# Attention, routed experts and a two-layer network on one core: the product of the last 64 keys with V in two column halves

## The chip, the cores and the metric

The kernel runs on one core of a Trainium2 chip. The metric is the device time of one execution in microseconds; the time before is the median of three runs, 412.99 us (412.54 to 413.68). A profile of one further execution was taken by the hardware profiler, and all rows below come from it. The engines are named as the profile names them: PE is TensorE's matmul, PEld its weight load, DVE is VectorE, ACT is ScalarE, POOL is GpSimd, SP is SyncE, which issues most of the DMAs.

## The reference

Three stages follow each other. The change lies in the first.

```python
# attention, B = 2, H = 8 heads, S = 576 positions, D = 64
scores = scale * np.matmul(q, k.transpose(0, 1, 3, 2)) + bias   # bias: a small network of the relative position
attn = np.exp(scores - np.max(scores, axis=-1, keepdims=True))
attn = attn / (np.sum(attn, axis=-1, keepdims=True) + 1e-09)
x = np.matmul(attn, v)            # 576 keys: 4 blocks of 128 and a tail of 64
# a top-1 mixture of 8 experts with a capacity, then x -> leaky relu(x @ w_in) @ w_out
```

## The kernel before

**Units.** The attention is cut into 40 units: batch b, block c of 128 queries (c = 0 to 3, and c = 4 for the last 64 queries) and pair p of heads 2p and 2p+1. Four units, p = 0 to 3, make one block. The order of the blocks is written out by hand, as is the order of everything else: each engine runs its instructions in the order in which the code issues them.

**The loop.** Step n of the loop (line 1270) issues on PE: `s0(n+1)`, the scores of the next unit (`qk`, L333, into St); `tr(n)`, the transposes of the exponentials A of unit n (L366 for the four full key blocks, L370 for the 64 tail keys of both heads together); one bias matmul group (L182, four column groups of 32 into pb) as long as there are any; the pieces that finish a block (`fin_b`, L441 and L449 behind the fourth unit, `fin_c`, L458 one step later); then `pv(n-1)`, the product with V of the unit before; then, in the earlier steps, another bias group. DVE adds bias and scores and takes the extreme (`ttr`, L345, into sv), ACT takes the exponential (`expo`, L356), and DVE and ACT copy the transposes out of PSUM (`tr_evac`, AT and AX_). AT and AX_ of a unit are made one whole step before its `pv`.

**The bias.** The bias matmuls end in bs, which SP stores to memory (L222, scr) and loads back skewed as bt (L314), which `ttr` reads. The bias groups run out on the way: PE starts the last one at 114.1 us.

**The product with V.** For c < 4 the result xp of a unit is 128 x 128: head 2p in PSUM partitions 0 to 63, head 2p+1 in 64 to 127. The four full key blocks are eight matmuls of 64 columns, one for each head and block (L403), whose weights are a head's 64 columns of V. The tail is one matmul over all 128 columns (L399): AX_ holds the 64 tail keys of both heads interleaved in its 128 partitions, and vd holds V's tail rows spread the same way, with zeros where the other head's keys are. Each matmul in fp32 is two passes on PE, so the profile shows L399 as x2 and L403 as x16 in each unit. There are 32 units with c < 4. The other 8 (c = 4, L407 and L409) are not touched.

Of the kernel before, what the change touches and what calls it, by code (L numbers as in the profile page):

```python
# [26 lines left out]
NFULL = S // 128  # L27
# [47 lines left out]
def tile_attention_moe_mlp(ctx, tc, qc, kc, vc, wpk, cst, ctok, cap, wm, wo, out):  # L75
    nc = tc.nc
# [318 lines left out]
    def pv(c, p, ATs, Vs, xp):  # L395
        V, vt, vd = Vs
        AT, AX_ = ATs
        if c < NFULL:
            nc.tensor.matmul(xp[:, p, :], vd[:, p], AX_, start=True, stop=False)  # L399
            for t in range(NFULL):  # L400
                for j in range(2):
                    h = 2 * p + j
                    nc.tensor.matmul(xp[64 * j : 64 * j + 64, p, :], V[:, t, 64 * h : 64 * h + 64],  # L403
                                     AT[:, j, 128 * t : 128 * t + 128], start=False, stop=t == NFULL - 1)
        else:
            for t in range(NFULL):
                nc.tensor.matmul(xp[:, p, :], V[:, t, 128 * p : 128 * p + 128], AT[:, 0, 128 * t : 128 * t + 128],  # L407
                                 start=t == 0, stop=False)
            nc.tensor.matmul(xp[:, p, :], vt[:, 128 * p : 128 * p + 128], AX_[0:64], start=False, stop=True)  # L409
# [860 lines left out]
    for n in range(N + 1):  # L1270
# [9 lines left out]
        if n + 1 < N:  # L1280
            b, c, p = units[n + 1]
# [12 lines left out]
        if n >= 1:  # L1294
            b, c, p = units[n - 1]
            pv(c, p, ATt.pop(n - 1), Vt[b], xpt[b, c])
            if p == NP - 1:
                fa = (b, c) + fin_a(c, rst[b, c], xpt[b, c], n == N)
# [71 lines left out]
```

## Time and profile before

| | |
|---|---|
| median of three runs | 412.99 us (412.54 to 413.68) |
| the profiled execution, its own time | 412.21 us |
| its span, first to last instruction | 410.3 us |
| TensorE busy | 381.2 us, 93% |
| VectorE busy | 309.2 us, 75% |
| ScalarE busy | 241.3 us, 59% |
| L399 / L403 | 32 x 2 and 32 x 16 passes, between 42.8 and 205 us |

A busy PE in this profile is not a PE at its peak: rows overlap, and the time that a group takes is best read as the distance from its first start to the start of what follows it. A row of the timeline merges instructions of one line that stand in a row; its first two columns are the start and how long it lasts, xN is how many passes it holds, and a bracket is the idle time before it and what ended that.

### The profile page before, as it was taken

To read this page: it belongs to the slowest core of one execution; us is meant where nothing else is said; L and a number is where in the kernel's file an instruction comes from. 1 tells how busy PE (TensorE), PEld (TensorE's weight loads), DVE (VectorE), ACT (ScalarE), POOL (GpSimd) and SP (SyncE) were. 2 spreads that over 40 slices of the span, in tenths; PEclk is the share of its full clock that TensorE was granted. 3 is DMA by queue.
4 is the path that set the end of the run, shared out by engine and by line. 5 is a ranking of instruction groups with operands and counts; after the bars stand their busy time and mean duration, and the time that the engine had idled before them with its cause. 6 is when DMAs were issued, how large, how long until landed. Compare 5 with 4: busy or idle time off the path is not lost. (4 is left out here: it accounts for less than half of the span.)

```text
span 410.3 us, 8306 instructions
## 1 busy us (share of the span) xinstructions
PE 381.2 (93%) x2926; PEld 316.8 (77%) x2926; DVE 309.2 (75%) x736; ACT 241.3 (59%) x519; POOL 139.4 (34%) x110
## 2 busy tenths in 40 slices
PE   4886999998899999999999999998999999899993
PEld 2244566666588988998988999998998778789872
DVE  5998988799855689799548883128989999999310
ACT  2756897697865777767565785546554222455200
POOL 1444857374300011031241304850233255222311
PEclk9999899999999999999998999999899999999998
DMA  8989599698779847788285189692344366630011
GB/s 194 332 254 334 173 322 326 203 316 270 199 218 320 297 150 224 224 269 196 95 235 208 41 306 366 218 316 81 140 137 172 103 201 206 208 106 1 12 66 51
DMA packets 34370, 82.97 MB, mean 202 GB/s; under 512 B 8491, under 2 KB 8875, under 8 KB 32272
## 3 DMA queue, kind: packets, MB, share of 16 engines
q1 hardware_dynamic: 33200, 79.88, 61.1%
q0 software_dynamic: 1120, 2.48, 1.7%
q8 instruction: 25, 0.41, 0.4%
q14 instruction: 25, 0.20, 0.1%
HBM read 60.29 MB, written 23.20 MB: 203 GB/s over the span
## 5 line engine op out<-in xcount | busy, mean ns | idle before, releaser
L345 DVE CUSTOM_DVE_ANT_0 sv<-St,bt 128x576 f32<-128x576 f32 x72 | 52.9, 750 | 32.9 <-PE St L333 21.9
L677 POOL TENSOR_TENSOR P<-raw,P 128x1024 fp32r<-128x1024 f32 x18 | 45.4, 2523 | 77.4 <-ACT P L676 70.2
L356 ACT ACTIVATE A<-sv,mx 128x576 f32<-128x576 f32 x72 | 59.2, 837 | 3.2 <-DVE mx L345 3.1
L333 PE MATMUL St<-K,Q 128*128 128x320 f32 (+1 forms) x320 | 53.5, 309 | 2.5 <-DVE mx L345 2.4
L182 PE MATMUL pb<-Gt,WP 128*32 128x272 f32 (+17 forms) x352 | 43.1, 509 | 13.2 <-DVE Gt L165 8.4
L333 PEld LDWEIGHTS St<-K,Q 128*128 128x128 f32 x320 | 43.9, 189 | 14.5 <-issue 9.8
L273 POOL TENSOR_TENSOR Q<-qr,Q 128x256 fp32r<-128x256 f32 x22 | 17.0, 772 | 103.0 <-ACT Q L265 63.2
L165 DVE TENSOR_SCALAR Gt<-WL,bp 128x432 f32<-128x432 f32 (+17 forms) x101 | 49.4, 549 | 0.1
L676 ACT CAST P<-raw 128x1024 fp32r<-128x1024 f32 x27 | 28.3, 1048 | 27.8 <-DVE raw L694 22.2
L366 PE MATMUL pt<-CS,A 128*128 128x128 f32 x288 | 41.6, 284 | 1.5 <-ACT A L356 0.8
L376 ACT COPY AT<-pt 128x512 f32<-128x512 f32 x40 | 23.4, 584 | 30.9 <-PE pt L366 30.8
L366 PEld LDWEIGHTS pt<-CS,A 128*128 128x128 f32 x288 | 38.0, 206 | 2.4 <-ACT A L356 1.3
L169 POOL TENSOR_SCALAR Gt<-WL,bp 128x528 f32<-128x528 f32 (+12 forms) x17 | 34.3, 2023 | 9.3 <-PE pb L182 9.2
L182 PEld LDWEIGHTS pb<-Gt,WP 128*32 128x32 f32 x352 | 13.2, 112 | 30.5 <-DVE Gt L165 14.3
L403 PE MATMUL xp<-AT,V 128*64 128x128 f32 x512 | 35.9, 284 | 0.0
L193 ACT ACTIVATE bs<-pb,CS 128x288 f32<-128x288 f32 (+53 forms) x60 | 27.3, 501 | 12.4 <-PE pb L182 7.9
L861 PE MATMUL g<-yhl,P 128*128 128x304 f32 x96 | 30.3, 316 | 2.8 <-DVE gfa L886 2.8
L1198 PE MATMUL ac<-P,hq 128*128 128x512 f32 (+1 forms) x80 | 31.5, 394 | 0.0
L1196 PE MATMUL ac<-P,hq 128*128 128x512 f32 (+1 forms) x80 | 31.5, 394 | 0.0
L1197 PE MATMUL ac<-P,hq 128*128 128x512 f32 (+1 forms) x80 | 31.5, 393 | 0.0
L403 PEld LDWEIGHTS xp<-AT,V 128*64 128x64 f32 x512 | 28.0, 139 | 4.0 <-issue 0.2
L894 DVE TENSOR_TENSOR hq<-gfa,hq 128x304 fp32r<-128x304 f32 x32 | 28.8, 901 | 1.4 <-ACT hq L893 1.4
(322 smaller groups left out, 913.9 us busy)
## 6 DMA issues: line engine op xcount, KB each, us to landing
bt<-scr SPq DMA_DIRECT2D x24, 576.0 KB, 5.7
w<-wo SPq DMA_DIRECT2D x13, 1024.0 KB, 5.1
scr<-bs SPq DMA_DIRECT2D x36, 295.5 KB, 5.0
raw<-wm SPq DMA_DIRECT2D x14, 512.0 KB, 6.5
w<-wm SPq DMA_DIRECT2D x10, 512.0 KB, 5.2
srt<-pre SPq DMA_DIRECT2D x6, 771.0 KB, 9.7
qr<-qc SPq DMA_DIRECT2D x16, 256.0 KB, 5.9
kr<-kc SPq DMA_DIRECT2D x12, 288.0 KB, 7.0
```

Of the source, the lines that this page charges most:

```text
L165: nc.vector.tensor_scalar(G, src, bp[:, g : g + 1], 0.0, op0=ALU.add, op1=ALU.max)
L169: nc.gpsimd.tensor_scalar(G, src, bp[:, g : g + 1], 0.0, op0=ALU.add, op1=ALU.max)
L182: nc.tensor.matmul(pb[32 * q : 32 * q + 32, 0 : hi - lo], W2, gs[:, q, lo:hi], start=True, stop=True)
L333: nc.tensor.matmul(St[:, o + lo : o + hi], Q[:, h - 2 * p, w, :], K[:, h - 2 * p, lo:hi], start=n == 0, stop=n == len(seq) - 1)
L345: nc.vector.tensor_tensor_reduce(out=sv, in0=St, in1=bt[:, jb], scale=-0.125, scalar=3.0e38, op0=ALU.add, op1=ALU.min, accum_out=mx)
L356: nc.scalar.activation(A[:, :, j], sv, AF.Exp, bias=mx, scale=-1.0, accum_out=rs[:, col : col + 1])
L366: nc.tensor.transpose(pt[:, 128 * t : 128 * t + 128], A[:, 128 * t : 128 * t + 128, j], ident)
L403: nc.tensor.matmul(xp[64 * j : 64 * j + 64, p, :], V[:, t, 64 * h : 64 * h + 64], AT[:, j, 128 * t : 128 * t + 128], start=False, stop=t = ...
L677: eng.tensor_tensor(out=P_[:, 1], in0=raw, in1=P_[:, 0].bitcast(F32), op=ALU.subtract)
L1196: nc.tensor.matmul(ps, hh, wh, start=k == 0, stop=False)
L1197: nc.tensor.matmul(ps, hh, wl, start=False, stop=False)
L1198: nc.tensor.matmul(ps, hl, wh, start=False, stop=k == F2 // 128 - 1)
```

## The change

`pv` no longer issues the 128-column tail matmul ahead of the eight others. Behind them it issues two of 64 columns, one for each head: the weights are that head's half of vd's columns, the moving operand is the same AX_ for both, and the result is added to that head's half of xp. The first matmul of each head (key block 0) now starts the sum, and the tail ends it. Nothing else differs on any engine.

```diff
         if c < NFULL:
-            nc.tensor.matmul(xp[:, p, :], vd[:, p], AX_, start=True, stop=False)
-            for t in range(NFULL):
+            for t in range(NFULL + 1):
                 for j in range(2):
                     h = 2 * p + j
-                    nc.tensor.matmul(xp[64 * j : 64 * j + 64, p, :], V[:, t, 64 * h : 64 * h + 64],
-                                     AT[:, j, 128 * t : 128 * t + 128], start=False, stop=t == NFULL - 1)
+                    w, a = (V[:, t, 64 * h : 64 * h + 64], AT[:, j, 128 * t : 128 * t + 128]) if t < NFULL else (vd[:, p, 64 * j : 64 * j + 64], AX_)
+                    nc.tensor.matmul(xp[64 * j : 64 * j + 64, p, :], w, a, start=t == 0, stop=t == NFULL)
```

On PE, in a unit with bias matmuls (the first of the places, at 49 us in the trace), the columns are the line, the operation, out<-in by name, and the shape of the result:

```order
 L182 MATMUL pb<-Gt,WP 32x400 x4
-L399 MATMUL xp<-AX__500,vd_95 128x128
-L403 MATMUL xp<-AT,V 64x128 x8
+L403 MATMUL xp<-AT,V 64x128 x8
+L403 MATMUL xp<-AX__500,vd_95 64x128 x2
 L182 MATMUL pb<-Gt,WP 32x416 x4
 L333 MATMUL St<-K,Q 128x320
```

The 128-column matmul stood between matmuls of 32 and of 64 columns; now the ones of 32 and of 64 columns follow each other directly.

On PE, in a unit without bias matmuls (at 119 us in the trace), before:

```order
L366 MATMUL pt<-CS,A 128x128 x8
L370 MATMUL pt_1606<-CS,A 128x128
L458 MATMUL pl_1625<-CS,lt 128x128
L399 MATMUL xp<-AX__1531,vd_96 128x128
L403 MATMUL xp<-AT,V 64x128 x8
L333 MATMUL St<-K,Q 128x320
```

and the same place in the changed kernel, whose lines behind L399 are one lower (L457 is L458 of before):

```order
L366 MATMUL pt<-CS,A 128x128 x8
L370 MATMUL pt_1619<-CS,A 128x128
L457 MATMUL pl_1638<-CS,lt 128x128
L403 MATMUL xp<-AT,V 64x128 x8
L403 MATMUL xp<-AX__1543,vd_96 64x128 x2
L333 MATMUL St<-K,Q 128x320
```

Here the 128-column matmul followed others of 128 columns; the step from 128 to 64 columns, which came behind it, now comes ahead of the V products.

## Rows read from the trace of the kernel before

**Rows 1.** The page: busy us, share of the span, number of instructions.

```profile
PE 381.2 (93%) x2926; PEld 316.8 (77%) x2926; DVE 309.2 (75%) x736; ACT 241.3 (59%) x519; POOL 139.4 (34%) x110
```

**Rows 2.** Stretches: length, busy us of each engine, granted clock, DMA share, GB/s.

```profile
core 0: us, PE busy (x) PEld busy (x) DVE busy (x) ACT busy (x) POOL busy (x), PEclk, DMA share, GB/s
...
54.00:71.00 17.00, 17.00 (x160) 10.67 (x159) 15.94 (x38) 15.07 (x35) 10.88 (x8) 1.00 0.99 325
...
79.40:111.00 31.60, 27.35 (x265) 19.19 (x266) 31.01 (x86) 26.50 (x60) 16.42 (x14) 1.00 0.87 266
111.00:206.00 95.00, 94.83 (x908) 84.19 (x905) 69.47 (x240) 66.86 (x174) 14.03 (x21) 1.00 0.73 224
```

**Rows 3.** PE timeline of a unit with bias matmuls: start, us, line, operation, count.

```profile
48.51 0.27 PE L370 MATMUL pt<-CS,A 128*128 128x128 f32 x1
48.71 0.88 PE L182 MATMUL pb<-Gt,WP 128*32 128x400 f32 x8
49.52 0.49 PE L399 MATMUL xp<-AX__500,vd 128*128 128x128 f32 x2
49.94 1.09 PE L403 MATMUL xp<-AT,V 128*64 128x128 f32 x16
50.96 0.91 PE L182 MATMUL pb<-Gt,WP 128*32 128x416 f32 x8
```

**Rows 4.** PE timeline of a unit without bias matmuls.

```profile
119.39 0.27 PE L370 MATMUL pt<-CS,A 128*128 128x128 f32 x1
119.49 0.27 PE L458 MATMUL pl<-CS,lt 128*128 128x128 f32 x1
119.60 0.39 PE L399 MATMUL xp<-AX__1531,vd 128*128 128x128 f32 x2
119.92 1.09 PE L403 MATMUL xp<-AT,V 128*64 128x128 f32 x16
```

**Rows 5.** PE by line, 109 to 206 us: busy us, mean ns | idle.

```profile
L403 PE MATMUL xp<-AT,V 128*64 128x128 f32 x336 | 23.0, 279 | 0.0
...
L399 PE MATMUL xp<-AX__1395,vd 128*128 128x128 f32 x2 | 0.5, 326 | 0.0
...
L399 PE MATMUL xp<-AX__1531,vd 128*128 128x128 f32 x2 | 0.4, 275 | 0.0
```

**Rows 6.** PE timeline of the first unit, then the clock granted in stretches.

```profile
42.80 0.80 PE L399 MATMUL xp<-AX__431,vd 128*128 128x128 f32 x2
43.52 1.98 PE L403 MATMUL xp<-AT,V 128*64 128x128 f32 x16
45.43 1.02 PE L182 MATMUL pb<-Gt,WP 128*32 128x464 f32 x8
...
42.20:45.50 3.30, 3.30 (x26) 2.15 (x26) 3.27 (x10) 2.83 (x7) 3.20 (x3) 0.50 0.69 196
219.60:223.00 3.40, 3.40 (x17) 3.33 (x16) 3.21 (x14) 1.26 (x2) 1.02 (x1) 0.51 0.97 379
```

**Rows 7.** Timeline of PE, ACT, SP and DVE: the chain from 68 to 79 us.

```profile
68.62 1.07 PE L182 MATMUL pb<-Gt,WP 128*32 128x512 f32 x8
69.76 0.91 ACT L193 ACTIVATE bs<-pb,CS 128x80 f32<-128x80 f32 x2 [1.51 <-PE pb L182]
70.69 0.32 SPq L222 DMA_DIRECT2D scr<-bs  x1
75.39 1.40 SPq L314 DMA_DIRECT2D bt<-scr  x3
79.43 0.76 DVE L345 CUSTOM_DVE_ANT_0 sv<-St,bt 128x576 f32<-128x576 f32 x1 [2.06 <-DMA bt<-scr]
```

**Rows 8.** Stretches around the store of that chain; then all stores of scr (page, issues).

```profile
57.00:70.00 13.00, 13.00 (x123) 8.21 (x118) 12.94 (x31) 11.15 (x27) 8.86 (x7) 1.00 1.04 347
70.00:72.00 2.00, 2.00 (x21) 1.83 (x23) 0.96 (x4) 1.78 (x4) 2.00 (x1) 1.00 0.62 227
...
scr<-bs SPq DMA_DIRECT2D x36, 295.5 KB, 5.0
```

**Rows 9.** Waits behind 111 us: PE to 206 us, DVE at 164 us, PE behind 205 us.

```profile
PE pt L366 <- ACT A L356: 0.2, 1, 0.2
...
164.34 0.76 DVE L345 CUSTOM_DVE_ANT_0 sv<-St,bt 128x576 f32<-128x576 f32 x1 [0.28 <-PE St L333]
...
PE g L861 <- DVE gfa L886: 2.8, 4, 0.9
```

## Prediction, made before the changed kernel ran

> **What bounds the kernel now.** I read the page first, for the busiest engine. It is PE [rows 1], but a share over the whole span says nothing of one stage, so I next read the stretches of the attention, where the changed matmuls lie. There the reader should see three regimes [rows 2]. From 54 to 71 us PE is never idle, and DVE nearly never. From 79.4 to 111 us DVE is busy 31.01 of 31.60 us and PE only 27.35: PE waits for DVE and ACT there. From 111 to 206 us PE is busy 94.83 of 95 us and DVE 69.47, and the one wait of PE is 0.2 us [rows 9]. So a shorter product with V is worth its full length behind 111 us, nothing between 79.4 and 111, and ahead of that only what reaches the DMA on which the middle stretch hangs. Third I read PE's timeline for what one unit pays [rows 3, 4], and last the chain of that DMA [rows 7].
>
> **What a tail matmul costs now.** I measure from start to start. Neighbouring passes of 128 columns stand (119.60 - 119.39) / 2 = 0.105 us apart [rows 4], but the last one ahead of matmuls of 32 columns takes 0.20 us [rows 3]: a change of width costs 0.095 us. Behind the bias matmuls the tail takes 49.94 - 49.52 = 0.42 us [rows 3]: two passes (0.21), the change of width (0.095) and about 0.11 for a weight load of 128 columns that nothing covers. Behind matmuls of 128 columns it takes 119.92 - 119.60 = 0.32 us [rows 4], which is the same without that load.
>
> **What the two halves cost.** The sixteen passes of 64 columns take 50.96 - 49.94 = 1.02 us. Taking off the change of width behind them (0.095) and half a weight load ahead (0.055, an estimate from the 0.11 for twice the columns) leaves 0.87 us for eight pairs, 0.109 us each: the two heads' passes run side by side. The halves add two pairs, 0.22 us. Upper bound: the halves read the same AX_ columns, which no pair of before does, and should that keep them apart they are four passes, 4 x 0.109 = 0.44 us. Lower bound: below 0.22 there is nothing, since a pair already runs at one 128-column pass. I take 0.22, because everything but the shared operand is as in the sixteen.
>
> Here a rule speaks against the change. The row says that eight pairs with their loads fit in 1.02 us [rows 3]. The Trainium skill, in "TensorE: Matmul & The Clock Gate", Part 3, section The mechanism, says that a weight load overlaps running matmuls only if it goes to other rows of the array. All these loads fill the same rows. By that rule each pair would show its load, 0.109 + 0.055 = 0.164 us, and eight would need 1.31 us; the trace has 1.02 and does not bear it out. I keep it as the fourth rival below.
>
> **The balance of one unit.** Behind matmuls of 32 columns (L182 or L449): minus 0.42, plus 0.22, a gain of 0.20 us. The step from 32 to 64 columns, which takes the place of the step from 32 to 128, has no row; I take the same 0.095 for it, as the steps from 64 to 32 and from 128 to 32 both show, and without it the gain would be 0.295. Behind matmuls of 128 columns the change of width is not saved but moved ahead: minus 0.32, plus 0.095, plus 0.22, which is a gain of 0.005 us, in effect nothing.
>
> **How many of each.** The mean length of L399 tells them apart: 326 ns behind narrow matmuls, 275 ns behind wide ones. Between 109 and 206 us there are 6 of the first kind (the first at 110.34 us, AX__1395) and 15 of the second, 21 units for the 336 passes of L403 [rows 5]. Gain: 6 x 0.20 + 15 x 0.005 = 1.3 us. The cover that could be lost is DVE's slack: in its tightest wait on a gaining unit, at 164.34 us, DVE still idles 0.28 us for PE [rows 9], more than the 0.20. Behind 205 us PE waits only where it and DVE chase each other (2.8 us in four places) [rows 9], and both start from work that PE released, so I let the shift run through to the end.
>
> **Ahead of 79 us.** The first unit runs at half the clock [rows 6]: L399 takes 0.72 us, and two more pairs at twice 0.109 cost 0.44; of the 0.28 I take 0.2, since bias matmuls slide into the slow stretch. Four more units ahead of 68.62 us (the first at 49.52 us [rows 3]) gain 0.20 each, one with wide neighbours nothing. PE is thus 1.0 us early at 68.62 us. From there: bias matmuls, ACT's copy, the store, the load, and DVE's wait of 2.06 us that ends at 79.43 [rows 7]. ACT had waited 1.51 us for PE, so the store is issued 1.0 us earlier. Between the store's issue and the load's lie 4.7 us. The DMA engines were full from 57 to 70 us, at a share of 1.04, and are at 0.62 in the next two [rows 8]. If the store waits behind that backlog, nothing is gained; if not, 1.0 us is. All stores have a median of 5.0 us [rows 8], so 4.7 is no sign of either. I take half, 0.5 us, with 0 and 1.0 as ends.
>
> **From 79.4 to 111 us** four more narrow units gain 0.8 us on PE. I count it at nothing: DVE's 31.01 us of work hide it. If that cover were gone it would be 0.8 us more.
>
> **Waits that move.** L399 was where PE first needed AX_; now the last pair needs it. AX_ was copied one whole step before, so neither waits, and no other queue is touched: no DMA is issued, moved or dropped, and the orders on DVE, ACT, POOL and SP stay as they are. ACT's copy of xp behind the fourth unit waits for the end of `pv`, which comes earlier.
>
> **Sum.** 1.3 + 0.5 = 1.8 us. The profiled execution took 412.21 us, which gives 410.4; the median of the runs is 0.8 us higher, 412.99, and 1.8 us off that is **411.2 us**.
>
> **Rivals.** (1) DVE takes the bound. The early 1.0 us is lost in the DMA backlog, and behind 111 us DVE, at 69.47 of 95 us, fills up around the ends of blocks where it has the most to do; the slack of 0.28 us at 164.34 [rows 9] is not far from 0.20, and a later one may be eaten by what came before. With half of the 1.3 lost as well, 412.4 us. For it: DVE's slack is thin. Against it: PE's single wait of 0.2 us in 95.
>
> (2) The halves do not run side by side, because both draw the same AX_ columns. Then each unit pays 0.44 us for its tail: narrow units lose 0.02, wide ones 0.44 + 0.095 - 0.32 = 0.215, so behind 109 us 15 x 0.215 + 6 x 0.02 = 3.3 us slower, **416.3 us**. It decides from 0.28 us for the two halves up: 6 x (0.42 - x) + 15 x (0.225 - x) is zero there. For it: no pair of before shares its operand. Against it: all other pairs do run together.
>
> (3) The change does not do what it says, the narrow step costing what the wide one did with its load: 413.0 us. Against it: the load of 64 columns takes less in the row of sixteen.
>
> (4) Each added pair shows its load: 0.33 us for the halves, so narrow units gain 0.09 and wide ones lose 0.105, 15 x 0.105 - 6 x 0.09 = 1.0 us slower, 414.0 us. The rule of the skill above would give this; the 1.02 us speak against it.
>
> **How the numbers follow.** My forecast, 1.3 us with an early part between 0 and 1.0 us, has a chance of 0.62, and its own range is 410.6 to 411.8. Rival 1 has 0.26, rival 2 has 0.06, rival 3 has 0.03 and rival 4 has 0.03. The range of 8 in 10 takes in rival 1 and at its lower end a narrow step that costs less than 0.095: 410.3 to 412.6. Where PE falls to half the clock is not mine to place: 219.6 to 223 us ran at 0.51 [rows 6], and a shift of 1.8 us may move such a stretch onto other work; it stays within that range. A difference of over 0.3%, 1.24 us, is about what a measurement of this kernel can tell from no change. Faster by more: 0.60, nearly all of the forecast. Within: 0.33, rival 1, rival 3, rival 4's lower part and the forecast's upper edge. Slower by more: 0.07.
>
> **What would show it.** Right: in units with bias matmuls the distance from the first V pass to the next group grows from 1.02 to 1.24 us, with L182 directly ahead of it; at 119 us PE's distance from L458's successor (L457) to the scores is unchanged within 0.02 us; DVE stays full from 79 to 111 us; and PE's lead at 206 us exceeds its lead at 111 us by 1.3 us. The early part is read at the wait that ended at 79.43: earlier by 0 to 1.0 us. Wrong: twenty passes that take 1.45 us (rival 2), new idle time of PE behind 111 us with DVE ahead of it (rival 1), or a lead at 206 us that is gone at the end.

## The result, and the profile after

| | before | after |
|---|---|---|
| median of the runs of this comparison | 413.34 us (412.54 to 414.23, 4 runs) | 409.88 us (409.4 to 410.45, 4 runs) |
| ratio | | 0.9916 [0.9891, 0.9942] |
| the profiled execution | 412.21 us, span 410.3 | 410.08 us, span 408.2 |

The changed kernel is faster by 3.5 us, 0.8%; three further comparisons gave ratios of 0.9876, 0.994 and 0.9923. The forecast was 1.8 us, and 409.88 lies below its range. The two profiled executions differ by 2.1 us only; why one pair of profiles shows less than the runs is taken up below.

**One unit.** PE's timeline of the changed kernel at the two places of [rows 3] and [rows 4] (start, us, engine, line, operation, count, idle before; lines behind L399 are one lower than before):

```profile
48.98 0.27 PE L370 MATMUL pt<-CS,A 128*128 128x128 f32 x1
49.18 0.88 PE L182 MATMUL pb<-Gt,WP 128*32 128x400 f32 x8
49.99 1.09 PE L403 MATMUL xp<-AT,V 128*64 128x128 f32 x16
50.92 0.39 PE L403 MATMUL xp<-AX__500,vd 128*64 128x128 f32 x4
51.23 0.56 PE L182 MATMUL pb<-Gt,WP 128*32 128x416 f32 x4
...
117.05 0.27 PE L370 MATMUL pt<-CS,A 128*128 128x128 f32 x1
117.16 0.27 PE L457 MATMUL pl<-CS,lt 128*128 128x128 f32 x1
117.36 1.09 PE L403 MATMUL xp<-AT,V 128*64 128x128 f32 x16
118.28 0.39 PE L403 MATMUL xp<-AX__1543,vd 128*64 128x128 f32 x4
118.60 0.53 PE L333 MATMUL St<-K,Q 128*128 128x320 f32 x2
```

The twenty passes take 51.23 - 49.99 = 1.24 us where the sixteen took 1.02, and the 0.42 ahead of them [rows 3] is gone: 0.20 us gained. The four passes of the halves, with the step to 32 columns behind them, take 51.23 - 50.92 = 0.31 us. At 117 us the step from 128 to 64 columns costs 117.36 - 117.16 = 0.20 us, and the unit is as long as before: 0.20 + 1.24 = 1.44 us against 0.105 + 0.32 + 1.02 [rows 4].

**The stretches.** Where the middle and late stretches of [rows 2] lie now, each moved by PE's lead there (columns as there):

```profile
78.00:109.60 31.60, 28.11 (x303) 19.82 (x294) 31.26 (x88) 27.21 (x62) 16.11 (x14) 1.00 0.86 270
...
109.60:204.00 94.40, 94.23 (x948) 83.22 (x947) 69.47 (x242) 67.55 (x177) 14.64 (x22) 1.00 0.72 221
```

DVE is still full in the middle stretch (31.26 of 31.60 us), and PE has 0.17 us of idle time behind it.

**The chain.** SP and DVE, the same steps as in [rows 7]:

```profile
70.42 0.32 SPq L222 DMA_DIRECT2D scr<-bs  x1
73.58 1.48 SPq L314 DMA_DIRECT2D bt<-scr  x3
...
77.57 0.76 DVE L345 CUSTOM_DVE_ANT_0 sv<-St,bt 128x576 f32<-128x576 f32 x1 [0.44 <-PE pt L366]
```

Here is the surprise. The loads of bt are issued 3.16 us behind the store instead of 4.70, and DVE's wait has gone from 2.06 to 0.44 us, although the store itself is only 0.27 us earlier (70.42 for 70.69). (The bracket names PE, but by the trace's semaphore events the load lands at 77.44 us, 0.13 us ahead of DVE, as in the trace of before with 79.30 and 79.43: it is the load that ends this wait in both, and by the same 0.13 us in e5, e6, e13, e14 and e16, whatever their brackets name.) Part of the small shift is the start: score unit 3 (counted from 0; the texts on record call it the third), from which I measure below because the start-up differs by up to 2.8 us between the profiled executions, began at 46.38 us before and at 46.86 after. From it to the end of DVE's wait passed 33.05 us before and 30.71 after, 2.3 us less, and to the first expert matmul 172.6 us before and 169.0 after. The 2.3 us have two parts: measured from unit 3 the store is issued 0.75 us earlier (23.56 us behind it for 24.31), and the loads follow the store 1.54 us sooner.

**Behind the attention.** The waits of PE from 205 us on (line waited for, us, times, longest):

```profile
PE g L860 <- DVE gfa L885: 3.1, 4, 0.9
PE g L727 <- DMA xr<-srt: 1.5, 1, 1.5
```

The second is new against [rows 9]: the rows of the second expert block arrive after PE wants them. PE leads the trace of before by 2.15 us at 112 us and by 3.1 from 204 to 217 us, but by 2.1 at 248 and at the end.

### The profile page after: what moved, and what is told of

Read it like the earlier page. It is cut to its first block, busy times and chain, and to the rows that moved or that the text cites. A ratio compares the mean times of both kernels' runs of the same rounds, so it can differ in the third digit from the quotient of the medians.

```text
span 408.2 us, 8432 instructions
## 1 busy us (share of the span) xinstructions
PE 377.8 (93%) x2990; PEld 313.4 (77%) x2990; DVE 308.3 (76%) x736; ACT 241.1 (59%) x519; POOL 139.3 (34%) x110
## 5 line engine op out<-in xcount | busy, mean ns | idle before, releaser
L165 DVE TENSOR_SCALAR Gt<-WL,bp 128x432 f32<-128x432 f32 (+17 forms) x101 | 48.4, 540 | 0.1
L675 ACT CAST P<-raw 128x1024 fp32r<-128x1024 f32 x27 | 28.3, 1048 | 28.8 <-DVE raw L693 22.2
L403 PE MATMUL xp<-AT,V 128*64 128x128 f32 x512 | 35.0, 279 | 0.0
L1197 PE MATMUL ac<-P,hq 128*128 128x512 f32 (+1 forms) x80 | 31.5, 394 | 0.0
L1195 PE MATMUL ac<-P,hq 128*128 128x512 f32 (+1 forms) x80 | 31.5, 394 | 0.0
L1196 PE MATMUL ac<-P,hq 128*128 128x512 f32 (+1 forms) x80 | 31.5, 393 | 0.0
```

Source lines behind the costliest of these rows:

```text
L165: nc.vector.tensor_scalar(G, src, bp[:, g : g + 1], 0.0, op0=ALU.add, op1=ALU.max)
L403: nc.tensor.matmul(xp[64 * j : 64 * j + 64, p, :], w, a, start=t == 0, stop=t == NFULL)
L1195: nc.tensor.matmul(ps, hh, wh, start=k == 0, stop=False)
L1196: nc.tensor.matmul(ps, hh, wl, start=False, stop=False)
L1197: nc.tensor.matmul(ps, hl, wh, start=False, stop=k == F2 // 128 - 1)
```

## Experiments

A product of 32 x 32 adds four rows to PE's stream; "halves" are the two passes that the change adds.

**One stretch of units at a time** (e1, e2, e3): the halves only in the units whose number is at most 5, 6 to 10, or at least 11 (`new` is that condition on n - 1, and what follows it is the changed kernel's loop).

```diff
+        if c < NFULL and new:
+            for t in range(NFULL + 1):
...
+        elif c < NFULL:
-        if c < NFULL:
             nc.tensor.matmul(xp[:, p, :], vd[:, p], AX_, start=True, stop=False)
```

> The two halves only in the first six units (pv up to 73 us in the trace of before), the other 26 units as before. Theory A (the early part passes in full through the bias store and the load of bt, so that DVE starts its full stretch earlier): 1.0 to 1.9 us faster than before, and DVE's wait that ended at 79.43 us ends at 78.5 us or earlier. Theory B (a backlog of the DMA engines sets when that store lands, and the wait of the changed kernel was short by chance): 0 to 0.4 us faster.

> The two halves only in units 6 to 10 (pv from 78.9 to 104.7 us in the trace of before), where DVE was full. Theory A and B: PE saves 0.8 us on four narrow units and only waits longer for DVE and ACT, within 0.3 us of before. Theory C (DVE is full there only because PE hands it work late): 0.6 to 1.0 us faster.

> The two halves only from unit 11 on (pv behind 109 us): six narrow units at 0.20 us and fifteen wide ones at nothing. All shifts pass through to the end: 1.2 to 1.3 us faster. Rival (the second expert block waits at about 241 us for rows that the scatters on GpSimd wrote, which PE's lead does not move): 0 to 0.5 us faster, with a wait of PE at the transposes of that block.

Against 413.51 us of before: 412.0 (0.9971 [0.9948, 0.9994]), 413.93 (0.9997 [0.9967, 1.0027]) and 412.35 us (0.998 [0.9955, 1.0006]). The middle part is worth nothing that the runs can tell, as the prediction had it. The early part is worth 1.2 us, as theory A has it and more than the 0.5 I had given it; DVE's wait ends at 78.05 us in e1. The interval of the late part takes in nothing as well as what was expected; its trace says more. In it the way from score unit 13 to the first expert matmul is 111.46 us, as in the changed kernel (111.44), against 112.62 before: the late part is 1.2 us, and PE's lead grows there in six steps of 0.2 us, one in each narrow unit.

**The kernel before again** (e4), one execution:

> The kernel before, once more, for a second trace of it. If the wait for bt at 79.43 us, the half clock at 219.6 us and the time at which the rows of the second expert block land are fixed parts of the kernel, they come again within 0.3 us; if they are of one execution, they differ by a microsecond and more.

412.99 us, and the chain as in [rows 7]: store to load 4.81 us, DVE's wait 2.37, score unit 3 to DVE 33.36, to the first expert matmul 172.6. The long way from store to load is no accident of one execution. The half clock at 219.6 us did not come again, and PE waited 1.58 us for the rows of the second expert block, for which it does not wait in the trace of before.

**What stands in that way.** PE's instructions come by DMA. The page of the changed kernel lists them as a queue of their own (packets, MB, share of 16 engines):

```profile
q8 instruction: 25, 0.41, 0.4%
```

Each packet holds 16 KB. The kernel before has 25 of them for its 5852 rows of PE and PEld, some 235 rows each, and 236 rows added to the changed kernel take its 25 to 26 (e6 and e14 below). One runs for 0.9 to 2.4 us in the traces, on one of the 16 DMA engines. In the kernel before, one of them starts at 71.75 us, 1.06 us behind the store on which bt hangs; the DMA of the way from store to load (busy tenths of 16 engines in 40 slices, then the queues):

```profile
DMA  3433101979998500100000001010000030000000
...
q1 hardware_dynamic: 193, 0.40, 22.2%
q8 instruction: 1, 0.02, 2.4%
```

The store's packets fill the slices from 71.5 us on, and by the packets' own times those of all other engines are through at 73.2 us; what is left is one engine, which runs eight packets of the store from 73.51 to 74.65, behind the fetch that ended at 73.53. (The trace does not name a packet's engine; that these eight share theirs with the fetch is read from the times.) SP waits for all of them. The halves add four rows in each unit, 20 by then, so the packet is fetched earlier: when it starts, 906 rows of PE and PEld have begun in the kernel before and 915 in the changed one. That is theory F: the fetch's place against the store is part of the early gain. Rival P: PE's lead alone is.

**The fetch moved by work in the bias groups** (e5: 24 rows into the kernel before; e6: 236 rows into the changed one, which with the 20 make 256, what I took for a packet; e10: 240 rows into the kernel before). N is 6 in the first bias group for e5, and 5 (in e6's twelfth group 4) in each of the first twelve for e6 and e10.

```diff
+            for _ in range(N):
+                nc.tensor.matmul(pb[0:32, 0:32], W2, gs[:, 0, lo : lo + 32], start=True, stop=True)
             for q in range(4):
```

> The kernel before with 6 tiny matmuls (32 columns, overwritten by the next one) ahead of the very first bias group, where PE mostly waits: 24 more PE instructions in the profile's count, no other change; the products with V are those of before. Theory F (a 16 KB fetch of PE's instructions sits on one DMA engine just as the last bias store of the second block needs it, 1.8 us from 71.75 us; the halves put more instructions into each unit and so moved that fetch about a microsecond earlier, ahead of the store): the fetch moves from 1.0 us behind the store's issue to about its issue, the wait from the store's issue to bt's issue falls from 4.2 to 4.7 us to 3.0 to 3.6, and the kernel is 0.8 to 1.3 us faster without any halves. Theory G (the store lands earlier because PE issues it earlier): nothing moves, within 0.3 us of before.

> The changed kernel with 59 such tiny matmuls in the first twelve bias groups: 236 PE instructions, which with the 20 that the halves add up to that place makes one whole fetch of 256. Theory F: the fetch is back where it was in the kernel before, the wait from the store's issue to bt's issue is 4.2 to 4.7 us again, DVE's wait for bt is about 1 us longer than in the changed kernel, and the gain over before is 0.8 to 1.3 us less than that of the changed kernel. Theory G: as fast as the changed kernel, less at most 0.5 us for the tiny matmuls themselves.

> The changed kernel once more, for a narrower interval and a second trace. Theory F: PE's lead at the first matmul of the first expert block is 3.0 us over before again, the store's wait is 3.0 to 3.6 us again, and the median is 2.8 to 3.5 us below that of before. If the first result was in part chance: 1.8 to 2.5 us.

> The kernel before with 60 tiny matmuls in the first twelve bias groups: 240 PE instructions, so that the fetch near the last bias store comes 16 instructions, about 0.8 us, later than in the kernel before. Theory F (it is the meeting of the fetch with that store on one DMA engine): the fetch now comes behind the store's packets, and the wait from the store's issue to bt's issue falls to 2.8 to 3.6 us although PE is not a moment ahead. Rival (earlier fetches help in themselves): 4.2 to 4.7 us and more.

Times: e5 412.26 (0.9941 [0.9919, 0.9964]), e6 412.03 (0.9932 [0.9905, 0.9958]), the changed kernel on the same chip (e7) 409.62 (0.9876 [0.9847, 0.9906]), e10 412.92 (1.0002 [0.9978, 1.0026]). In place, the way from store to load moves as F says in all: 2.82 us in e5, 4.33 in e6, 3.39 in e7, 2.23 in e10, where the fetch came only behind the store's landing (e5 and e10 went lower than I had expected; and in e6 the fetch started 2.19 us behind the store, not 1.06, so it is not back at its old place). In time e5 gained 2.4 us where F had 0.8 to 1.3, e6 lost 2.3 against e7 where F had 0.8 to 1.3, and e10 shows nothing. All three kernels with added products ran the start-up with 6.8 us of half clock in one piece in their profiles, where no stretch of half clock in another profile was longer than 3.4 ahead of 400 us, and their score unit 3 starts at 48.2 to 48.9 us, at 46.1 to 47.7 in all others. So their added work is not neutral, and their times do not price the fetch.

**The place and the width apart** (e8: the halves ahead of the V products; e9: the whole 128-column product, but behind them).

```diff
 e8
-            nc.tensor.matmul(xp[:, p, :], vd[:, p], AX_, start=True, stop=False)
+            for j in range(2):
+                nc.tensor.matmul(xp[64 * j : 64 * j + 64, p, :], vd[:, p, 64 * j : 64 * j + 64], AX_, start=True, stop=False)
 e9
-            nc.tensor.matmul(xp[:, p, :], vd[:, p], AX_, start=True, stop=False)
...
+            nc.tensor.matmul(xp[:, p, :], vd[:, p], AX_, start=False, stop=True)
```

> The two halves ahead of the eight products with V, in the place of the matmul over all columns, instead of behind them. If the gain is the change of width and the bare weight load (as predicted) and not the place: twenty passes in 1.24 us as in the changed kernel, and the same time within 0.5 us. If the place counts (a wait for AX_ there): PE idle ahead of the halves, and slower than the changed kernel by that.

> The tail matmul over all 128 columns, as before, but behind the eight V products: the place alone, with the same number of PE instructions, so that the fetches of instructions stay where they were. If the gain is the width of the halves, not their place: PE's distance from the last bias group to what follows the product is 1.44 us as before, DVE's wait for bt ends as in the kernel before, and the time is within 0.3 us of before. If the place counts: 0.5 us and more faster.

e8: 410.87 us, 0.9895 [0.9861, 0.993]; with e7 on the same chip, at 0.9876 [0.9847, 0.9906], there is no difference to tell. Its twenty passes take 52.07 - 50.83 = 1.24 us too:

```profile
50.02 0.88 PE L182 MATMUL pb<-Gt,WP 128*32 128x400 f32 x8
50.83 0.44 PE L400 MATMUL xp<-AX__500,vd 128*64 128x128 f32 x4
51.10 1.04 PE L404 MATMUL xp<-AT,V 128*64 128x128 f32 x16
52.07 0.91 PE L182 MATMUL pb<-Gt,WP 128*32 128x416 f32 x8
```

e9: 412.21 us, 0.9992 [0.9962, 1.0021], anything from 1.6 us faster to 0.9 slower. So the width alone brings the gain, and the place alone brings too little for these runs to tell. e9's timeline shows what the place does:

```profile
50.64 1.09 PE L402 MATMUL xp<-AT,V 128*64 128x128 f32 x16
51.67 0.49 PE L404 MATMUL xp<-AX__500,vd 128*128 128x128 f32 x2
52.09 0.91 PE L182 MATMUL pb<-Gt,WP 128*32 128x416 f32 x8
...
115.73 1.09 PE L402 MATMUL xp<-AT,V 128*64 128x128 f32 x16
116.76 0.49 PE L404 MATMUL xp<-AX__1468,vd 128*128 128x128 f32 x2
117.00 1.32 PE L333 MATMUL St<-K,Q 128*128 128x320 f32 x8
```

Ahead of bias matmuls the tail still costs 52.09 - 51.67 = 0.42 us, as in [rows 3]. Only where scores follow, which are 128 wide too, it costs 0.24. That is why e9 gains in the late part, where scores follow every tail: 111.57 us from score unit 13 to the experts, 112.62 before, in the same six steps of 0.2 us as with the halves. There the place alone brings what the width brings; in the early part it brings PE nothing (score unit 8 starts 29.35 us behind unit 3, 29.16 before and 28.39 after). Its profiled execution is 2.1 us shorter than that of before on the way from score unit 3 to the experts. 1.05 us of this is the late part, and most of the rest is DVE's wait for bt, which I had expected unchanged: 1.10 us instead of 2.06, as the fetch starts 1.03 us behind the store, much as before, but takes 1.18 us instead of 1.77. Twelve executions do not show that part.

**A delay behind the attention** (e11: the changed kernel with twelve products of the first down group run once more, 1.6 us of PE, ahead of it; e12: the changed kernel beside it).

```diff
...
             k = 2 * j + kk
+            for m in range(NP if more else 0):
+                mm3(acs[m][:, 0:n], Pt, 512 * kk + 128 * m, h_(0, k, n), h_(1, k, n), True, True)
             for m in range(NP):
...
```

> The changed kernel with 12 repeated matmuls (1.6 us of PE at full clock) ahead of the first down product of the first expert block; they are overwritten. If the second expert block waits for rows that the scatters on GpSimd bring, PE's time in the first block has slack of 0.8 to 1.6 us: the distance from the first matmul of the first expert block to the transposes of xr is 25.2 to 26.5 us as without them, and the kernel is at most 0.8 us slower than the changed one. If PE sets that time: 1.6 us slower.

> The changed kernel a third time, beside the three others on the same chip: 3.0 to 4.5 us faster than before; the time from the third group of scores to the end of DVE's wait for bt 30.7 to 31.2 us, against 33.0 to 33.4 before; from the score group at 111 us to the first expert matmul 1.0 us less than before.

Both have a median of 410.54 us (0.9952 [0.9925, 0.998] and 0.994 [0.9916, 0.9964]), so the delay costs nothing that the runs can tell; e12 gains 2.5 us where I had expected 3.0 to 4.5. PE's timeline shows where the 1.6 us went, first the wait in the changed kernel:

```profile
240.00 0.29 PE L862 MATMUL ac<-hq,P 128*128 128x288 f32 x1
241.78 1.34 PE L727 MATMUL g<-CS,xr 128*128 128x128 f32 x8 [1.49 <-DMA xr<-srt]
```

and the same place in e11:

```profile
241.89 0.29 PE L862 MATMUL ac<-hq,P 128*128 128x288 f32 x1
242.57 0.66 PE L727 MATMUL g<-CS,xr 128*128 128x128 f32 x4 [0.38 <-DMA xr<-srt]
```

From the first expert matmul to these transposes pass 25.95 us in the one and 25.85 in the other: the added work fills the wait. The transposes wait for rows loaded behind a chain of POOL's scatters, each of which waits for the one before to land:

```profile
223.17 1.02 POOL L567 DMA_INDIRECT srt<-xn,sl  x1 [4.48 <-DMA srt<-xn,sl]
...
227.08 0.98 POOL L567 DMA_INDIRECT srt<-xn,sl  x1 [2.66 <-DMA srt<-xn,sl]
231.29 0.97 POOL L567 DMA_INDIRECT srt<-xn,sl  x1 [3.23 <-DMA srt<-xn,sl]
```

The chain's length differs between executions. The wait was 1.49, 0.80 and 0.16 us in three traces of the changed kernel (e12 the second, e7 the third), none in a fourth (e16), none in the trace of before and 1.58 us in e4. So PE's lead is not always passed on whole: in the pair of profiles 1.0 of 3.1 us is gone behind this place, which is most of what they show less than the runs.

**The fetch alone** (e13: five products of 32 x 32 in the 5.65 us in which PE has nothing to do at the start, in the kernel before; e14 and e15: 59 and 32 of them in the changed kernel; e16: the changed kernel beside them). For them the memset of `ones` on POOL moves to the front, and pd takes one turn of the PSUM buffers that the transposes use; score unit 0 starts at 28.6 to 28.8 us in all four profiles.

```diff
+    pd = ps_t.tile([128, 512], F32, name="pd", tag="pt")
+    for _ in range(N):
+        nc.tensor.matmul(pd[0:32, 0:32], ones[:, 0:32], ones[:, 0:32], start=True, stop=True)
```

> The kernel before, with five products of 32x32 (20 rows of TensorE) ahead of everything, in the 5.65 us in which TensorE has nothing to do yet. Nothing else is changed: no halves, no other place of the tail product. The 20 rows are as many as the halves add up to the score unit at 70 us. Theory F (the fetch of TensorE's instructions lies on the chain to DVE's wait): the fetch that starts at 71.75 us in the kernel before starts about 1 us earlier against the last bias store, the store's landing to the issue of the loads of bt falls from 4.7 us to 2.8 to 3.7, the distance from the third score unit to DVE's wait for bt from 33.1 to 31.5 to 32.2, and the time is 1.0 to 1.6 us under the kernel before (ratio 0.996 to 0.9975). Rival P (TensorE's lead alone does it): 33.1 as before, ratio 1.000 within 0.2%.

> The changed kernel, with 59 products of 32x32 (236 rows) in the same idle time at the start, so that with the 20 rows of the halves the fetch stands where it does in the kernel before (256 rows are one packet). Theory F: store to issue of bt 4.2 to 4.8 us again, distance from the third score unit to DVE's wait 31.9 to 32.2 (the changed kernel: 30.7 to 31.2), time 1.0 to 1.5 us over the changed kernel of the same chip, so a ratio of 0.994 to 0.996 to the kernel before. Rival P: as the changed kernel, 0.9905 to 0.992.

> The changed kernel with 32 such products (128 rows) at the start: the fetch stands half a packet away, neither with the store nor right behind it. Theory F: store to issue of bt 2.2 to 3.0 us, DVE's wait there 0 to 0.3 us (0.44 in the changed kernel), so at most 0.4 us better than the changed kernel, if the other fetches hit nothing. Rival P: no difference to the changed kernel of the same chip.

> The changed kernel as it is, on the chip of the three others: 409.5 to 410.5 us, ratio 0.989 to 0.994 to the kernel before; it is what the two kernels with rows at the start are compared with.

From store to load all three did what F says; e14's way from unit 3 to DVE's wait, 34.57 us where 31.9 to 32.2 were expected, is taken up below. SP and DVE in e13, store, load and DVE's wait:

```profile
70.55 0.32 SPq L225 DMA_DIRECT2D scr<-bs  x1
73.49 1.92 SPq L317 DMA_DIRECT2D bt<-scr  x3
...
77.73 0.76 DVE L348 CUSTOM_DVE_ANT_0 sv<-St,bt 128x576 f32<-128x576 f32 x1 [0.50 <-PE pt L369]
```

In e14, where the store was issued at 71.81, the load and the wait:

```profile
76.25 0.88 SPq L317 DMA_DIRECT2D bt<-scr  x2
...
80.64 0.76 DVE L348 CUSTOM_DVE_ANT_0 sv<-St,bt 128x576 f32<-128x576 f32 x1 [2.12 <-DMA bt<-scr]
```

And in e15, where DVE doesn't wait for it at all:

```profile
71.39 0.32 SPq L225 DMA_DIRECT2D scr<-bs  x1
73.66 1.39 SPq L317 DMA_DIRECT2D bt<-scr  x3
...
77.98 0.75 DVE L348 CUSTOM_DVE_ANT_0 sv<-St,bt 128x576 f32<-128x576 f32 x1
```

The whole set, in us behind the issue of that store, from the packets in the traces:

| kernel | fetch starts | fetch ends | bt issued | end to issue | DVE's wait |
|---|---|---|---|---|---|
| before, e4 (before), e2, e3 | 1.07, 1.06, 1.06, 0.99 | 2.84, 2.97, 2.53, 2.73 | 4.70, 4.81, 4.36, 4.58 | 1.86, 1.84, 1.83, 1.85 | 2.06, 2.37, 2.08, 2.09 |
| after, e7, e12, e16 | 0.34, 0.49, 0.14, 0.21 | 1.37, 1.52, 1.51, 1.35 | 3.16, 3.39, 3.55, 3.15 | 1.79, 1.87, 2.04, 1.80 | 0.44, 0.72, 0.95, 0.58 |
| e11 (after, up to there) | 1.27 | 2.30 | 4.10 | 1.80 | 1.91 |
| e13, e5 (before, moved earlier) | 0.27, 0.14 | 1.15, 1.02 | 2.94, 2.82 | 1.79, 1.80 | 0.50, 0.53 |
| e14 (after, moved back) | 0.97 | 2.67 | 4.43 | 1.76 | 2.12 |
| e6 (after, moved back) | 2.19 | 3.12 | 4.33 | 1.21 | 1.75 |
| e15, e10 (fetch elsewhere) | none within | | 2.26, 2.23 | | 0, 0 |

e1, e8 and e9, which are not in the table, lie at 2.38, 1.79 and 1.48 us behind the fetch's end. In 12 of the 16 traces with a fetch there the load is issued within 0.1 us of 1.8 us behind its end, and where none is near, 2.2 us behind the store. This settles the mechanism in place: the store waits behind the fetch. What counts is the fetch's end, and that is not set by its start alone: in the traces of before, e8 and e9 it starts 1.07, 0.92 and 1.03 us behind the store and ends at 2.84, 1.79 and 2.21, and the loads follow at 4.70, 3.59 and 3.69. Why one fetch takes twice as long as another is not shown.

In time it is not as clean. e13: 412.21 us, 0.9996 [0.997, 1.0021], which misses F's 0.996 to 0.9975 in its middle and only touches it, although its profile is 1.6 us shorter than that of before up to DVE's wait and 1.2 us up to the experts. e14: 412.42 us, 0.9989 [0.9967, 1.001], and on the same chip e16: 409.33 us, 0.9923 [0.9894, 0.9951]. Putting the fetch back cost 3.1 us, twice what F had and nearly the whole gain; the clock granted to the two kernels' runs is nearly the same (0.9845 and 0.9858 in the mean). e15: 410.25 us, 0.9941 [0.9921, 0.9961], no better than e16. All fetches move with the added rows, not this one alone, and e14's profile shows two more that hit a chain. DVE has two waits there that were 1.40 and 0.40 us in the trace of before (SP, ACT and DVE):

```profile
46.37 1.11 SPq L225 DMA_DIRECT2D scr<-bs  x2
51.61 0.37 SPq L317 DMA_DIRECT2D bt<-scr  x1
...
56.03 0.76 DVE L348 CUSTOM_DVE_ANT_0 sv<-St,bt 128x576 f32<-128x576 f32 x1 [1.91 <-DMA bt<-scr]
...
103.92 1.15 ACT L236 CAST K<-kr 64x1152 fp32r<-64x1152 f32 x1 [1.53 <-DMA kr<-kc]
...
105.10 1.42 DVE L283 TENSOR_TENSOR K<-kr,K 64x1152 fp32r<-64x1152 f32 x1 [1.52 <-ACT K L236]
```

The second of the two stores is issued at 47.16 us, and its load follows 4.45 us later, where the traces of before, after, e7 and e16 have 2.24 each. By the packets' times a fetch runs from 48.16 to 49.85, and eight packets of the store run behind it from 49.83 to 50.98, as in the kernel before at 73.5 us. The load of kr shows the same: a fetch runs from 99.83 to 102.23, and the last four packets of that load run one after the other from 102.21 to 103.42, the rest of it having been through at 101.86. Counted from score unit 3, e14's unit 13 starts 3.4 us later than e16's. The difference grows by 0.7 us at the first of these places, by 1.1 at the fetch that was meant and by 1.0 at the third; 0.4 more come right behind unit 3, where both ran at half clock.

So in this pair of profiles three fetches make up 2.8 us, and the one at 72.8 us is only one of them. What the fetch at 71 us is worth alone, in the time of the whole kernel, stays open: 0.2 us by e13's ratio, 1.2 to 1.6 us by its profile.

## Why the prediction was wrong

**Right: the units.** 0.20 us in narrow ones, nothing in wide ones, 1.24 us for twenty passes. Rivals 2, 3 and 4 fell with that row. (The prediction says that the step from 64 to 32 columns shows 0.095 us; its rows do not separate that step, the changed kernel's do: 0.31 us for the halves and the step, of which 0.22 for the halves leaves 0.09.) The rule weighed in the prediction and kept as rival 4 (the Trainium skill, "TensorE: Matmul & The Clock Gate", Part 3, section The mechanism, weight loads hidden only in other rows of the array) is not borne out here: pairs added in the same rows took 0.11 us each. The same section also names a background weight buffer as a way to hide a load, which no run here tells apart.

**Right: the middle.** The four units there brought nothing that the runs can tell (e2, 0.9997), with DVE full for 31.26 of 31.60 us.

**Right: behind 111 us.** The sum had 1.3 us; from score unit 13 to the experts it was 1.2 us (112.62 to 111.44), the same in e3 alone, 0.2 us in each of the six narrow units. Rival 1 fell: PE has no new wait there.

**Wrong: the early term.** The failing step is "I take half, 0.5 us, with 0 and 1.0 as ends", ahead of 79 us. From score unit 3 to DVE's wait the profiled pair shows 2.3 us, and the other traces of the changed kernel 0.9 (e11, with a late fetch) to 2.1. Both ends were drawn for one question: whether the 4.7 us between the store and the load would pass PE's lead on. That part was right, near its upper end: the store came 0.75 us earlier behind unit 3, where the four units in between have 0.8, and all of it reached DVE. But both ends took the 4.7 us itself as given. It was not: 1.5 us of it was a packet of PE's own instructions, and the change, by adding instructions, moved that packet.

The other traces say the same, less exactly. With the fetch moved but no halves (e5, e13) the way to DVE's wait is 31.5 us, 1.6 less than before. With the halves but a late fetch (e6) it is 32.0 us, 1.1 less. With both it is 30.7 to 31.9. e14, halves with the fetch put back, has 34.6; of this 1.5 us is half clock right behind unit 3, which takes 6.73 us there and 5.21 in the trace after, and 0.7 us is the first of the two other fetches, so some 32.4 us are left, an estimate, 0.6 less than before. The 31.9 is e16's, whose unit 3 takes 6.35 us for the same reason.

The prediction read the backlog of the DMA engines [rows 8] as the only thing that could hold the store up, and counted no DMA as moved by the change ("no DMA is issued, moved or dropped"). That sentence is the error in its plainest form: instruction fetches are DMAs, and a change in the number of instructions moves every later one of them.

**The sum.** 1.3 + 0.5 = 1.8 was expected. From score unit 3 to the experts the profiled pair has 3.6 us: 0.75 for the earlier store, 1.54 for the fetch, 1.18 behind unit 13 and 0.15 in between. The shorter units' own part of it, 0.75 + 1.18 = 1.9 us, is thus close to the forecast, and the fetch is what the forecast lacked. Five traces of the changed kernel give 2.1 to 3.6 us for this way, and up to 1.5 us of that can stay at the scatter chain; the four timed comparisons gave 2.5 to 5.1 us. The lower edge of the range, 410.3 us, came from the ends of the early term, and fell with them.

**What stays open.** How much of the 3.5 us is the fetches' places over the whole kernel, and how much the shorter units, in runs and not in profiles. e14 says that with other places nearly all of it goes (0.9989); e6, with the same number of rows in another place and a start-up of its own, kept 0.9932. The halves alone are thus worth between 0.1% and 0.7% by these two, and 0.5% (1.9 us) by the profiled pair. e13, in which only the fetch moves, did not get faster by more than its runs can tell. No version beat the changed kernel: e8 and e15 are as fast within what the runs can tell.

## What to carry to other kernels

Count the instructions that a change adds or drops on each engine, not only their time: they shift every later fetch, and one that falls just behind a store on a chain (here one 16 KB packet, 0.9 to 1.9 us at that place, on one DMA engine) can cost or bring nearly as much as the edit itself saves (1.5 us beside 1.9 in the profiled pair; in the runs it is open). When a trace shows an unusually long way from a store to the load that waits for it, look at which packets finished last and what ran ahead of them, before deciding whether the way is fixed. Where narrow and wide matmuls alternate, matching the width of what stands beside an operation saves the change of width and the uncovered weight load, whichever side it stands on.

## What was not expected of the hardware

- A change of the number of TensorE instructions by 20 in some 940 moved DVE's wait for a DMA by 1.5 us, with no instruction of DVE, SP or the queues changed (2.06 us in the trace of before, 0.50 in e13). In time the runs of e13 do not show it.
- The load of bt is issued within 0.1 us of 1.8 us behind the fetch's end in 12 of 16 traces, whether the fetch took 0.88 or 1.91 us.
- TensorE's granted clock falls to half (1.2 GHz) for 3.4 us at places that differ between executions of one program: at 42, 220 and 288 us in the trace of before, at 33 us alone in e4 (and in both at the very end). Where such a stretch fell right behind score unit 3, that unit took 6.35 to 6.73 us instead of 5.21 (e14, e15, e16). Single executions of the kernel before ran from 411.0 to 416.6 us.
- A chain of indirect scatters whose members each wait for the one before to land had steps of 3.9 to 5.5 us in the trace after; it made a gate at 242 us that PE's lead ran into.
